# Cross-shaped window attention on one core: another order for the same instructions

## The chip, the core and the metric

The kernel runs on one core of a Trainium2 chip. The metric is device time in microseconds (us) of one execution, taken as the median of several. In the profile PE is the matrix engine (PEld its weight loads), ACT the activation engine, DVE the vector engine, POOL the GpSimd engine, and SP the engine that here only issues DMAs.

## What is computed

The input is an image of 224 x 224 tokens with 96 channels, in bfloat16. Half of the channels attend within horizontal stripes of 8 rows, the other half within vertical stripes of 8 columns. That makes 28 + 28 stripes of 1792 tokens, each an ordinary softmax attention with 48 channels.

```python
q, k, v = split(einsum('bhwc,cd->bhwd', x, wqkv))      # 96 channels each
# first 48 channels: 28 stripes of 8 rows, 1792 tokens each
ah = softmax(einsum('bqc,bkc->bqk', qh, kh) * 48 ** -0.5)
oh = einsum('bqk,bkc->bqc', ah, vh)
# last 48 channels: 28 stripes of 8 columns, 1792 tokens each
av = softmax(einsum('bqc,bkc->bqk', qv, kv) * 48 ** -0.5)
ov = einsum('bqk,bkc->bqc', av, vv)
out = einsum('bhwc,cd->bhwd', concat(oh, ov), wo)
```

## The kernel before

**Tiling.** Two stripes are worked on at once and form a pair (28 pairs, `P`). One stripe of the pair lies in partitions 0 to 63, the other in 64 to 127. The queries of a pair are cut into chunks of 512, 512, 512 and 256 (`CH`), the keys into blocks of 128. A unit is 128 keys against a chunk of queries, for both stripes.

**Units.** For a unit, PE multiplies keys and queries (line 778, `ps<-QT_sb,KT_sb`) in two steps, each of which fills one 512-column bank of PSUM. Then the scores must be exponentiated, and there are two ways:

- 984 units go to ACT: one activation (line 824) turns two banks into the tile `PT`. Then two PE steps multiply `PT` with the values (line 804, `ps<-PT,V_sb`).
- 388 units (776 banks) go to DVE: one instruction per bank (line 844) writes integers into `I_sb`, whose bits are read as bfloat16 numbers, a coarse exponential. POOL adds constants to them and makes two shifted copies, `U_sb` and `E_sb` (line 849). PE multiplies all three with the values, so such a unit has six steps on line 804.

A chunk's products pile up in one bank; DVE copies the sum into `OT_sb` (line 870), PE multiplies that with `wo` (lines 691 and 725), DVE divides by the softmax sum (lines 695 and 729), and for the vertical stripes POOL adds the horizontal half from `Ph_sb` (line 733). SP stores the result (line 760). Beside that, the next pair is projected: PE lines 535 and 637, DVE lines 549, 556 and 642, POOL lines 573, 574 and 651; SP fetches its input (lines 411 and 418).

**Tiles of the matrix engine.** All these matmuls use a 64 x 64 quarter of PE. A step works on two quarters at once, one for each stripe: either the two on the diagonal (`mode="q"`) or the two off it (`mode="v"`). A step of either kind can run beside a step of the other kind. Which kind a step is depends on the unit alone.

**Order.** Nothing is scheduled when the kernel is built. A string `SEQ` has one letter for each operation of the whole kernel, 11,330 in all. Each letter takes the next operation of its stream: `a` and `b` are the key-query steps of an ACT unit and of a DVE unit, `A` the activation, `c` the value steps of `PT`, `j` DVE's exponential, `U` and `u` the making of a `U_sb` or `E_sb` tile on POOL or, for the small letter, on DVE, `d` and `D` the value steps of the DVE unit, `f` and `e` PE and DVE work of the projections, `o`, `g`, `r`, `q`, `y` the end of a chunk from the copy to the store, `X` the fetches. A second string, `BANK`, has the PSUM bank for each tile in the order in which tiles are begun.

```python
for c in seq:                                  # Work.run, cut
    both, q = c == "p", {"p": "P", "u": "U"}.get(c, c)
    op = s.streams[q][at[q]]
    at[q] += 1
    deps = list(op.deps)
    for t in op.take + op.book:
        if t.k is None:
            t.k = int(next(digits))            # a digit of BANK
            t.after, freed[t.k] = freed[t.k], None
    ...
    s.place(op, deps)                          # next on its engine, with semaphore waits
    for t in op.give:
        freed[t.k] = [op]
```

So `SEQ` sets the order on each engine, and with `BANK` it sets which earlier operation a step must wait for before it may write into a bank. An engine takes its instructions in that order, and one that waits for a semaphore holds up those behind it on its engine.

Of the kernel before, what the change touches and what calls it, by code (L numbers as in the profile page):

```python
# [23 lines left out]
def ndc(P, c):  # L24
# [4 lines left out]
    "HiIxIihIiHiIhiiiihIiHiiihxIiiiIhiIiixhhxhxhxhhihHhxihhHhhhhhexhHhhxefHfxHfeexeaaxefAaxeafxAeaaxcebcAajabVccAja"  # L29
    "accbexdAacjacbdAjbcacajxbUAacacjbAjbcacajbxUAacjacbddAjacxacffAUeacacebeDAcaejacDAeacuacfAaafcecAecaacfoAaaeff"  # L30
    "cAceaadkgdfAkfradrXadbdeAdfaDaDejbcfcAcjaUcaXcbecAfadadjdfdfAaDeaDUbDXDfAjdadacebcAdcXdajadbdcADucacacDjbAUcac"
    "ajcbcAccjcaadobdADaDajbffdfAjdaUbadedfAcjacacfcecAbacUacegjcAbcacardjbdAdardadVddjdADbDaDjaDbcAdUcjacacbcdAcja"
    "cacDbDAoaUdadjgdAadarDdrbdDAcdjabUadcDjcAaaccbcDcjbAacacjUccgcAaoadrdbrDgADadarjdfdUAdarcacfecAgacaecfcdAUraDr"
    "aDDbDeAfcacajdbdAdaedadjdbkdAckadjUadbDcDAXXjacaccbcAjcbaaccUjcccAfadoadffADfaDeadbdUeAdgjdacacbrcAarcacfjcdbA"
    "UceacadfjdfAadbdadjbfAXcacaeDUdDdDAXjdadafDcADceabacDUcjAcbacacjbcAcoaacjbAgadadrjfUdfADfaDraddfedAaceacbfVcAe"
    "cacajcbdAdjbadaUddjbAddacajcdDbADaDjaDcbUcdAjacacbccDAjabaccDjUbdAacadjdbcAjadadcbocdAUDdadjagDdAcrDgracacDrcA"
    "brcUacacjcccAaoaddbDgAajdaUdfdrdArbDacaecfcAcjagacUcreADbDaDarDfcAdajdadfdeAUdDadacedcAdbdadjaDbcAXXjackacUbcc"
    "AjbacaccjcccAaadokdbUDAjbadaddgjdbAafrDjacffAUracacecfbcAcaejcacfcAdaudadffeAXdfadeaddDAXbdafjacdDAdeabaDDDjcb"
# [12 lines left out]
    "cjbAcDcajcacDcAagcUoacrbArdaadjgdbdAdarjDagDArdaUcarcfrcAcacaecbcfcAjDaDaDebDAadadjfddfAdeaUdacdcedAbdadjaDbDc"
    "AXXjackacUbccAjbcacaccjcfAaadodfkDfAUbDaedadgdjAdfacacerbcrAacUacjcbdfdAjadadbdeddAacjbdacDdjAXabUaDDdjDbAXcDj"
    "aDabcjcAfacUaccfcfAaceaccccbAoaadUdfjDAadadedffAadaDfbfUceAcacaecfcAceadajdbdVAdjbaDaDDjbADDacacjUdbddAjacgadc"
    "rcAbrcacacdjcUbAcacjacdbDAoadadjcgAUbadrajddcdADdrabadDjDcADgUacarcbrcAacacjcbccAcjaUadodbADajDadggdArbdradUac"
    "rjbcAdadardfdAcjacacfecUAcacaebfccAjadaddDedDAadafbdeDAXXDDDjackacUbcAcajcacbcccAjcfaadokdfUAdfadaedbdgcAjDaDa"
    "dfrdbArdUadaejdbdfAcjcacacbecAdcacajbdcdAXDjaUbaDdjDbAXDDaDjabccAjcacaUcffAcfcaeacccAcboadaUdfjdAgadaedffAdfra"
    "DraDcfUcAeabacecfcAcaeacjcbcAacVjbDaDDjbAdadadjbdUAadjbdaDdcjdcAbcacjaccdUAdbacajbcDDAaoaddjbDAgUDadardjdcdAcd"
    "radabcDAgjDUcacacrbcrAacacjcccAbodaUadjDgbDAardjadfddAragacUecbcAacrjacfccAracadefdUdAdaeaDDfDADDeabadDjbkAddU"
    "dadjabcdcAXXjacaccbcAajcakcbcccjcAUfadaodffAdadeadfgdAcrbecraDaDjfcAUcadeadbdfAdfjadadbcAcfjcacabecAXdUcaDjabd"
    "DdAXDjbadajDDDAcbUcacjacfcAcaceaccbcAoaUaddfjfAgfadeaddfdAraDraDVcfecAabaceccjbAcaUdajdbdAdajdadbDdADjbDaUDacj"  # L60
    "dcAbcacjacbcdAcjacaUbdcDAjbacacjcDbAdaoaddUdddjAcgcaacrcrdcAdabafcjDADDaecaUcDcbAcagjaccAroadardgUdbAdradjadbD"
    "ArDacajcbgAcUjacaccfrcAradaddfedAdfUaedacdDeAdDabaDdjbdDADakjDaUbccAXXjcacacbcAcjbacackjcccUAfadaodfcfAacaedgd"
# [872 lines left out]
```

## Time and the profile before

| | |
|---|---|
| median of 3 runs | 947.26 us (946.06 to 947.78) |
| profiled execution | 947.97 us |
| its span, first to last instruction | 945.8 us |
| PE busy | 935.8 us |
| ACT busy | 926.0 us |
| DVE busy | 883.1 us |
| POOL busy | 768.3 us |
| granted PE clock | 0.998 |

A row of groups on the page reads: line, engine, operation, tile written and tiles read, shapes, count; then the time in which at least one of the group ran, the mean duration of one in ns, and the idle time of the engine just before them with what ended it. Instructions of one engine overlap: the next begins while the last one drains, so durations add up to more than busy time. PE's ends are modelled, and a busy PE can still have one of its two tile pairs empty. A row of the waits reads: engine and tile that waited, what released it, us in total, times, the longest.

### The profile page before, as it was taken

The numbers are of one execution on the slowest core, as the hardware profiler recorded it, in microseconds if no ns is written. First come the engines' busy times: TensorE is split into PE (matmuls) and PEld (weight loads), VectorE is DVE, ScalarE is ACT, GpSimd is POOL, SyncE is SP. The second block draws the span as 40 slices with busy tenths as digits, with TensorE's granted clock in tenths as the row PEclk, the third lists the DMA queues.
The fourth block names the chain that finished last, engine by engine and source line by source line (L and its number), as shares of the span: only waits on it lengthen the run. The fifth ranks groups of instructions, "written<-read, shape, count | busy, mean of one in ns | idle before, by whom it ended". The sixth has DMA issues, their size and how long they took to land.

```text
span 945.8 us, 48282 instructions
## 1 busy us (share of the span) xinstructions
PE 935.8 (99%) x21770; PEld 641.5 (68%) x21770; DVE 883.1 (93%) x1755; ACT 926.0 (98%) x993; POOL 768.3 (81%) x511
## 2 busy tenths in 40 slices
PE   9999999999999999999999999999999999999997
PEld 4766767776677777667666766666776676677664
DVE  8999999999999999999999999999999999999994
ACT  7999999999999999999999999999999999999996
POOL 3789787888898887888888988887888787888883
PEclk9999999999999999999999999999999999999999
DMA  8804422440442243054210534545364544451112
GB/s 141 138 5 71 72 45 29 71 64 11 71 71 38 37 71 61 14 71 71 50 25 12 91 59 57 90 78 81 50 90 74 82 65 67 80 83 31 31 21 45
DMA packets 253254, 57.09 MB, mean 60 GB/s; under 512 B 252936, under 2 KB 252936, under 8 KB 253048
## 3 DMA queue, kind: packets, MB, share of 16 engines
q1 hardware_dynamic: 251464, 53.47, 36.0%
q8 instruction: 170, 2.79, 1.2%
q10 hardware_dynamic: 1584, 0.55, 0.3%
q14 instruction: 36, 0.29, 0.1%
HBM read 19.13 MB, written 28.21 MB: 50 GB/s over the span
## 4 chain that ended last, share of the span: by engine, by line
PE 97%; DVE 1%; DMA 1%; ACT 0%; issue 0%; POOL 0%; POOLq 0%; ACTq 0%
PE ps L804 50%; PE ps L778 36%; PE ps L535 5%; PE ps L637 4%; PE ps L691 1%; PE ps L725 1%; DMA w_sb<-in_wqkv_dram 1%; DVE I_sb L844 0%; ACT PT L824 0%; PE ps L602 0%; DVE out_sb L736 0%; PE ps L634 0%; POOL out_sb L733 0%; POOLq L302 0%; PE ps L529 0%
## 5 line engine op out<-in xcount | busy, mean ns | idle before, releaser
L824 ACT ACTIVATE PT<-ps 128x1024 bf16<-128x1024 f32 x984 | 922.0, 1034 | 7.6 <-PE ps L778 3.4
L778 PE MATMUL ps<-QT_sb,KT_sb 49*64 49x512 bf16 (+1 forms) x6272 | 740.2, 354 | 0.3
L844 DVE TENSOR_SCALAR I_sb<-ps 128x512 int16<-128x512 f32 x776 | 511.8, 684 | 21.0 <-PE ps L778 15.2
L804 PE MATMUL ps<-PT,V_sb 64*50 64x512 bf16 (+1 forms) x4496 | 498.3, 350 | 0.3 <-issue 0.3
L778 PEld LDWEIGHTS ps<-QT_sb,KT_sb 49*64 49x64 bf16 x6272 | 285.0, 105 | 144.5 <-ACT PT L824 44.4
L849 POOL TENSOR_SCALAR E_sb<-I_sb 128x2048 int16<-128x2048 int16 x168 | 319.1, 1900 | 51.8 <-PE ps L804 32.0
L849 POOL TENSOR_SCALAR U_sb<-I_sb 128x2048 int16<-128x2048 int16 x165 | 313.5, 1900 | 49.8 <-DVE I_sb L844 28.4
L804 PE MATMUL ps<-U_sb,V_sb 64*50 64x512 bf16 (+1 forms) x1776 | 245.3, 350 | 0.0
L804 PEld LDWEIGHTS ps<-PT,V_sb 64*50 64x50 bf16 x4496 | 217.7, 100 | 33.9 <-issue 1.0
L804 PE MATMUL ps<-I_sb,V_sb 64*50 64x512 bf16 (+1 forms) x1776 | 239.6, 352 | 0.2
L804 PE MATMUL ps<-E_sb,Vs_sb 64*50 64x512 bf16 (+1 forms) x1776 | 230.6, 349 | 0.0
L733 POOL TENSOR_TENSOR out_sb<-tmp,Ph_sb 128x480 bf16<-128x480 f32 (+1 forms) x84 | 85.7, 1030 | 26.2 <-DVE tmp L729 8.7
L804 PEld LDWEIGHTS ps<-I_sb,V_sb 64*50 64x50 bf16 x1776 | 80.8, 100 | 32.5 <-PE ps L804 9.3
L804 PEld LDWEIGHTS ps<-U_sb,V_sb 64*50 64x50 bf16 x1776 | 89.3, 100 | 12.5
L804 PEld LDWEIGHTS ps<-E_sb,Vs_sb 64*50 64x50 bf16 x1776 | 88.4, 100 | 13.6 <-issue 0.4
L535 PE MATMUL ps<-xa_sb,w_sb 64*64 64x512 bf16 (+3 forms) x440 | 79.9, 355 | 0.7 <-DMA w_sb<-in_wqkv_dram 0.7
L870 DVE CAST OT_sb<-ps 128x512 bf16<-128x512 f32 x112 | 69.1, 617 | 8.4 <-PE ps L804 7.9
L535 PE MATMUL ps<-xb_sb,w_sb 64*64 64x512 bf16 (+2 forms) x436 | 76.9, 348 | 0.0
L556 DVE TENSOR_SCALAR_CACHE_REDUCE KT_sb<-ps,bias 128x512 bf16<-128x512 f32 x108 | 71.6, 677 | 1.9 <-PE ps L535 1.5
L549 DVE TENSOR_SCALAR QT_sb<-ps 128x512 bf16<-128x512 f32 (+1 forms) x111 | 67.4, 616 | 3.7 <-PE ps L535 2.2
L637 PEld LDWEIGHTS ps<-w_sb,xa_sb 64*64 64x64 bf16 x1512 | 59.5, 109 | 10.9 <-DVE I_sb L844 4.0
L637 PE MATMUL ps<-w_sb,xa_sb 64*64 64x48 bf16 x1512 | 66.6, 187 | 0.1
(68 smaller groups left out, 610.4 us busy)
## 6 DMA issues: line engine op xcount, KB each, us to landing
x_blocks<-in_x_dram SPq DMA_DIRECT2D x54, 336.0 KB
out_dram<-out_sb SPq DMA_DIRECT2D x104, 42.0 KB
out_dram<-out_sb SPq DMA_DIRECT2D x208, 21.0 KB
out_dram<-out_sb SPq DMA_DIRECT2D x22, 24.0 KB
xa_sb<-x_blocks SPq DMA_TRANSPOSE x27, 5.0
xb_sb<-x_blocks SPq DMA_TRANSPOSE x27, 5.5
Ph_sb<-in_x_dram ACTq DMA_DIRECT2D x1, 336.0 KB, 3.3
out_dram<-out_sb ACTq DMA_DIRECT2D x6, 24.0 KB
```

What stands on the lines that cost most here:

```text
L535: ins = e.matmul(out_, lhsT=wt, rhs=rhs, start=i == 0, stop=startup or i == 1)
L549: return e.tensor_scalar(dst, src, QS if startup else A128, None, ALU.mult)
L556: return e.tensor_scalar(dst, src, bias[:, 0:1], None, ALU.add, ALU.add, accum_out=acc)
L637: ins = e.matmul(out_, lhsT=(xa_sb, xb_sb)[i][b][o:o + 64, 0, t0:t0 + 64], rhs=w2_sb[o:o + 64, i, wblk(P, "v"), 0:C2], start=i == 0, stop= ...
L691: ins = e.matmul(bk3[to:to + 64, s, :], lhsT=OT_sb[b][o:o + CA, blk * 64:(blk + 1) * 64], rhs=wo_sb[0][o:o + CA, :], start=True, stop=True)
L733: return e.tensor_tensor(res, tmp[t][:, 0:n, :], ph, ALU.add)
L778: ins = e.matmul(bank(t.k)[to:to + 64, i * qs:(i + 1) * qs], lhsT=KT_sb[b][64 * w:64 * w + CA, 64 * k:64 * k + 64], rhs=QT_sb[b][64 * w:64 ...
L804: ins = e.matmul(bank(k_.slot.k)[to:to + CP, 0:qs], lhsT=V_[o:o + 64, k, :], rhs=rhs()[o:o + 64, h * 512 + i * qs:h * 512 + (i + 1) * qs], ...
L824: a = wk.add("A", Op("act", ACT, lambda e: e.activation(split(PT[i % NPT]), two(ts), ACTF.Exp, scale=LN128), qs_ + pt_free.get(i - NPT, [] ...
L844: ds.append(wk.add("j", Op("dve", 0.6, lambda e, t=t, at=at: e.tensor_scalar(I_sb[y][:, at:at + 512], bank(t.k), one, 0.0, ALU.add, ALU.ma ...
L849: fn = lambda e, dst=dst, c=c: e.tensor_scalar(dst[:, 0:m], I_sb[y][:, 0:m], float(c), 1.0, ALU.add, ALU.mult)
L870: k.evac = wk.add("o", Op("dve", 0.07 + qs / 960, lambda e, k=k, b=P % 2, q0=q0, qs=qs: e.tensor_copy(OT_sb[b][:, q0:q0 + qs], bank(k.slot ...
```

## The change

Only the two strings differ. The letters are the same and as many, but for two tiles `U_sb` or `E_sb` that DVE makes instead of POOL (57 small `u` instead of 55). The first 12 and the last 4 letters agree. Two lines of the diff of `SEQ` show its kind:

```diff
 SEQ = (
-    "HiIxIihIiHiIhiiiihIiHiiihxIiiiIhIiiixhhxhxhxhhihHhxihhHhhhhhexhHhhxefHfxHfeexeaaxefAaxeafxAeaaxcebcAajabVccAja"
...
+    "HiIxIihIiHiIihiiihIiHiiihxIiiiIhIiiixhhxhxhxhhihHhxihhHhhhhhexhHhhxefHfxHfexeeaaxefAxaeaxfAeaaxcecbAaeaVccAjba"
...
```

On PE, just after the start: rows of line 778 are key-query steps, of line 804 value steps, and x2 is one step (a matmul for each stripe). Before:

```order
L778 MATMUL ps<-QT_sb,KT_sb 64x512 x4
L804 MATMUL ps<-PT,V_sb 50x512 x2
L778 MATMUL ps<-QT_sb,KT_sb 64x512 x2
L804 MATMUL ps<-PT,V_sb 50x512 x2
L778 MATMUL ps<-QT_sb,KT_sb 64x512 x6
L804 MATMUL ps<-PT,V_sb 50x512 x4
L778 MATMUL ps<-QT_sb,KT_sb 64x512 x4
L804 MATMUL ps<-PT,V_sb 50x512 x4
```

After:

```order
L778 MATMUL ps<-QT_sb,KT_sb 64x512 x4
L804 MATMUL ps<-PT,V_sb 50x512 x4
L778 MATMUL ps<-QT_sb,KT_sb 64x512 x6
L804 MATMUL ps<-PT,V_sb 50x512 x4
L778 MATMUL ps<-QT_sb,KT_sb 64x512 x6
L804 MATMUL ps<-PT,V_sb 50x512 x4
L778 MATMUL ps<-QT_sb,KT_sb 64x512 x2
L804 MATMUL ps<-I_sb,V_sb 50x512 x2
```

The two key-query steps of an ACT unit now mostly follow each other (523 of 984 units; 105 before), where a value step stood between them before (840 units before, 375 now). Over the whole of PE the places where the next step uses the other tile pair become fewer: runs of one step between such places go from 5287 to 2937, runs of two from 912 to 1396, runs of three or more from 176 to 595.

On PE, near the end, a place of before where four value steps stand ahead of two key-query steps (the names as above, `U_sb` and `I_sb` being tiles of DVE units):

```order
L778 MATMUL ps<-QT_sb,KT_sb 64x512 x4
L804 MATMUL ps<-PT,V_sb 50x512 x4
L804 MATMUL ps<-U_sb,V_sb 50x512 x2
L804 MATMUL ps<-I_sb,V_sb 50x512 x2
L778 MATMUL ps<-QT_sb,KT_sb 64x512 x4
```

And a place near the end of after:

```order
L778 MATMUL ps<-QT_sb,KT_sb 64x512 x6
L804 MATMUL ps<-PT,V_sb 50x512 x2
L804 MATMUL ps<-E_sb,Vs_sb 50x512 x6
L778 MATMUL ps<-QT_sb,KT_sb 64x512 x2
L804 MATMUL ps<-PT,V_sb 50x512 x4
L778 MATMUL ps<-QT_sb,KT_sb 64x512 x4
```

Such rows of several steps in a line are rare in before and common in after.

On POOL, the first tiles that it makes (with their buffer numbers; `Vs_sb` and `half`, `ksb` belong to the projections). Before:

```order
L651 TENSOR_SCALAR Vs_sb0<-V_sb0 128x1400
L849 TENSOR_SCALAR U_sb0<-I_sb0 128x2048
L849 TENSOR_SCALAR E_sb0<-I_sb0 128x2048
L849 TENSOR_SCALAR U_sb1<-I_sb1 128x2048
L573 TENSOR_TENSOR half<-ksum1 128x2
L574 TENSOR_TENSOR ksb1<-half 128x1
L849 TENSOR_SCALAR U_sb2<-I_sb2 128x2048
```

After:

```order
L651 TENSOR_SCALAR Vs_sb0<-V_sb0 128x1400
L849 TENSOR_SCALAR U_sb0<-I_sb0 128x2048
L849 TENSOR_SCALAR U_sb1<-I_sb1 128x2048
L849 TENSOR_SCALAR E_sb1<-I_sb1 128x2048
L849 TENSOR_SCALAR E_sb0<-I_sb2 128x2048
L573 TENSOR_TENSOR half<-ksum1 128x2
L574 TENSOR_TENSOR ksb1<-half 128x1
```

Which tiles fall to DVE changes, and POOL's tiles stand otherwise among the small steps of the projections. On SP the fetches of a pair now stand between single stores instead of behind all 24 of a pair. ACT runs the same activations in the same sequence; only what they wait for differs.

More of the change, by code (lines that the diff above doesn't have):

```diff
@@ L34 @@
[L34 to L38, printed above, removed]
@@ L129 @@
[L129 to L131 removed]
+    "HiIxIihIiHiIihiiihIiHiiihxIiiiIihIiixhhxhxhxhhihHhxihhHhhhhhexhHhhxefHfxHfexeeaaxefAxaeaxfAeaaxcecbAaeaVccAjba"
+    "acxcjbdAcajacbdAjbcacaxjbUAcacajbAjacacbxAfuacacjdAdcaxecaUbDDAjbacacjbAacjacUfAaceacefAeaeaecbcAacjacfoAuaaec"
@@ new lines @@
+    "cAadadbDfADjadXUadefdAdbafeacfjfAgcaecXakcbcrAckarDaDjbDfAcaceacjXcfbAaDUaddDdDeAUXdfafjafdAddaeacbdcdAjacaccb"
+    "cdcjbAacajcbcAaoadUdfDjADaadedffAgfdardaUecfAcracabcefcAaDaDeDVjbDADcaaddjdbcDdAajacdcdAddacaUUAacbccjcacbdcdA"
+    "cjacabodddaAdjadDgDAcdrdabraAdcDjcDbaajccfUcAcecaabcAcccjgadadrofUdAdaarddgcerbDAaacjDbcAdacjagdrdAbDaUdrabjcc"
+    "caArcaDfDjAddbUaecadAcDjdabadjcdcfAXXcUaeackbcDAcjbDaakcjcccAfaaDodbjdfAaUDaddfdcbAadaecgccaadAcjcbrrAfdUejdaa"
+    "dbdfAjcaadeDAbXcDcdcaUjaDbDdAXcjfafafcAedUbaaccdjAcDDbacjacccbAoaUacjbAgdaarjdfdAdadrUabdeADfDaajccfbfAdaedadf"
@@ new lines @@
+    "UAjdedaadcdbccdDDAaacdbcjaVAjcabcAdDDajUaccbAcDccjacacfDcAceaoUadADbDdaajcbcfdjdAddaeadUcgcdAgracracDDcAracrba"
+    "cUcccjaAbdaodfdAjdadadegbADDjacrabccAcjagacdcrbAUdarajddcAcrbadadfDjcAUbaecadDdjDDabdAajcdcfcAXaXceaUbcDcADjba"
+    "acjcccAfadoabddAfUDajadDfdgbAceaacrcckdbjAkdaarUAdjacdbcadfddcjbAacabecjDdUAdDXDajacDfAXcafafecfAUcdecabacAdDj"
+    "bcDcaajcbAcaUoacAjgbDaadrrdfDdAacajcfdfAedfabUaecdfAjdaaceAbddfadadVdddAcjaDceaDDbudADaacjbcdcAcajaccccbADuaac"
+    "cDbjcUAcajaddDdAobaaccjddbDdAajadgccAdragcUraADDrccbacarcjcccAbaUdaodfjAddedaaDbdgADcaajccrAbcfdrjacadcdAbacae"
@@ new lines @@
+    "dUfdjdAcbcaeaccdcAdjagaUDrDDAdardbjaDcAXXbajcaccfDAcUcaebacocfADjabadfjdfAdadaedkgkbADrcajcadAbrccaaDjbAddUjaU"
+    "ccbadfjAddDbaaedjbdAcDaXjuDaDdccfAXaaffecfAecdaacUbcAdjcDbacjaDbcAacajccUcAobaaddjdfAdaDaebDffUAdfjcaabdefAcac"
+    "jecacUAbcfdaaDeddbdjAbaadjcddccAjdaabDdDcAgaDVaccjcDdAracraDcAcbcadjabUdcUddAajaDDfocAdaaedcgcUAdcdragracDrccD"
+    "bcAaracjcccAUbaadodfjdADadeabddgcAajbaDccrjAbcccaarcfdUdAjadabcdefADDaaeDjUdbADjdaagcbcArajadcddrcAXXdbjaacbUD"
+    "cDAaacjcbcccAjcfaadodffaAaeddgdbAcrUDcajabkArDkccaUcjabdcfAjcadaecbdAddajbUacfdccjAXaedabfAXcfafjadUDDeAddabac"
@@ new lines @@
+    "DDjbAdccjaabUcDcAajcaoDcAbcbjagadUddraaAjdfrddADDaaebcfcfAUjcfacaedcbacdAajdfbddAaVacDddAddcajUecDaDdbcAjDaUca"
+    "cbcDcaAcjabcDccAjbaadDdoAfUdadaeccjAdDdgadacDbrrdAcUaaDcjcbcAjcacagccAcraoarbdAddgadadjbdArjUDDaagcrcbAcrcaajc"
+    "fAcddraUadebdfADaddjacDbeAaDajddcAcDfcaaUdcdfAXXceaacDcbecDAajbacccccAjafkadodfbDAajdaDbddfkAdajcUagcecAfcUaac"
+    "crcberfDDaAjaceAbDDcaUacfjdfAdXbjaadbdddfAXjadadcdecdAaUbacjDcbAccDajacbcAcjaUacboAaadjdfdbdaAdeUafdfAjDfabaDe"
+    "cfAjdaacUVebdcAcfdaaDdeadjDaAbdcdjDdADbcaacjcAcdbgjaUarcAccDcdcraacbcADcajcadUbdocaAcajdgdddADraraddUDfAcgacaD"
@@ new lines @@
+    "ercDcAcabcraUcAjcccabadodfADdaajddbdacaeADjbcfAjDDDaaceggdUAaDadrrbdcrdAajarccUdbfcaaAedccjdbAddjaacbcdcAXbXka"
+    "jaDcUjcDAbakcacjcbccAcfjaaddfoADfaUcDeabdcgAdjaadbcrAdfdacarUcejbAcfdjdaaedddbAdacaUccjbAXccjdabaDcdAcXjdfafUa"
+    "fDfAeccaDeaDDAbDcaajcUcbAcoaacjbAgddarajfdfAdfrUdaadbcbeaAajDDfcAjcacacbecfAdcaaceaDdbdbjAaddjVcdddAjaacdDUDAb"
+    "jcaaDbcAjcudacaccDDcaAcdaoadUdbADdjadDcdgAdcdarafrcUAcaceabjDcDAcbaacjccccUAagobdadrjdAdbaadrdfDADjcaacgceUcAb"
+    "agrcjacdcaArdadfrcraAUDabddedfAcaeDaDdDjbcbAkjdaaAcXXjddcabaDjccbDAakccjacbccAjUcfaadodfbUaAadjddfcDbAeaDadfjd"
@@ new lines @@
+    "bcAUaceacjfAdddaeabccgAjdaaUccrcbdADdaXraDdjDDfAXafafUdccbdAeUaaDjccAcbDcajabccAccajacboAdadjadfdAgaedaUdfDfAr"
+    "DfcaraccfeAdaeadddfAddeaabddcbcjAdajVcacbccAcaUajbcDAcdjDbaacjDDcDbAUaacjDcbAccajaAcdobcDUaDadfjcAdgdeaacddrAd"
+    "cacraUDbjDcbdAcjcaaccgcAoaUadbrdDrgAddarjaccAdbardacfjcAgaaUDcfrceAcaceacfdAdDraadedbbUdjcdaAadDjDbdDAajdabckj"
+    "kAXXdcbacaDjcbcAjDaUacbcccAjcfaadodfUdAbdajdadfAcbeaDacDgjcbAUccaajcfrdAdedrabaddfcdAjcaUabeacAXcjcdadDAbXDcjd"
+    "fUafafDdaADbeaDcjcDcAbaUjaccccbAoaacjbAgdaadrjfUDdadAraddffeADfcaabecfUAdjddaadbedfAcaecajccbDAbaadcjUAddjccca"
@@ new lines @@
+    "DbacjDbADaVcjadcbjccdcaaAccUbDDAoaaddjgaDAadrddrgcUAdDrdfrcaaAbdaeDacccDjcbaUAjacccbccAjcaadobdUAdaaddjggDrADb"
+    "racrajcAUdcbrcaacfAdjcadabddefAdjcaadDceDdAbUaaDjDdAbddDjaabcDAXXcjUcacabccfaccAjacecccAafoDadbdfDadAjUadkfdgA"
+    "ceacacbrjAcckcbaUracdfeAdjaaddbdfDddaAjabeDfcUAXacajbfcfAXadajddecDbAjacDacUbDcaAjcbacccdjcDAaabocUfaAddjagedf"
+    "AdfadrDadrfDAcbeaaccfjAcdacVaedbcfUAdacjaddedbAdacUjaccbcAdajaDcDdbcAaajcDdDcbAcaUcjacDbDAoadadjdgDAaadUDrrbAd"
+    "dcdajadbDcDAcjacgUacbrcAcracacjcccAaadodfUdAdgaeadDbArdDajgaccUrAcbaarjccdbdcaAadrdfjAdDDbaaeDDfAdjcaceacdUdbA"
@@ new lines @@
+    "jUdaadcfcADDXbXeacacbjkAckacacbjcccAcjfaaoddfDbAdaajddfUdgaAcearbcDcfArcaaecdjbcfAUcddaadjdeAbddcaajbcddAcXajb"
+    "acUjDcAdXfafafcDcbAaDaejDcUDbcDcAajacAccboaaddfjUbdAeadadffAfjaabeAdDDcfUaaccbjcceAcajaccfbcDDAeaacjbDDADdjaag"
+    "dDudbAdadradUddcccAaacjrbccdbAajadcVjAcUbadadobAjcDaaDdddjdcAagUdargDcrdAaaDccrcrbAcaaccjcccAobUaadjddgbAdDrad"
+    "adjfDAragUacecfcAcrceaacfArddaDadfedbAdaecacDjAcbDkaajcddAdbadjaUbkAXDXcdDDacjabccbAccajUacjccAcfaodadfDfADeUa"
+    "dagdcAbrcadradfjccbaAaeccjbccUaAdbajdfdAdjaaedddDbdaDAXjaDDfcfUAXafaeADbDdccUaabjcAccjcdabacccccAjbaadodfUAdaj"
@@ new lines @@
+    "adddfDfeAfDaabecfUcAdadjacbecfAdaeaddjddAVgacraccrbAdDajaDDcdbAjcuaacccbcDDAUjaaccDbdAcjacacodADbddaadjdbAcdDj"
+    "UaabDccjdAbaaDdjccAbaacjUccgcAcragraccAroaadrdgUbAdDadadrjDAdbragajcfcUAcraecacccAcbaraccfdjDAeaadbddfAjdacaeb"
+    "ddUADdafjadDDAXDXedbDacacbckUjaAcacjcbccjcAfaodadfdfAadadekbcUdgAcDaajfDrcecAbracacbdjfAUddjaadcdebdcAdajadbdA"
+    "XDjDaUbaDdDjAXcDfafafDAccbecaUaccbjcAajcacccAobcaadUdfjADdfaedaddffADaeagcfcrAVrbacacecAcaacfjcbcdAUaDeajddbAj"
+    "adcbdadjAUcddbDDaaDjbcAcjacabcjccDAUcDaabodbdAajaddgcAdjbaUaDDdrdAdjDraaddcccbjAcacUacbDcAjagacccrcAraadbUoddf"
@@ new lines @@
+    "dDADjaaedgdbAacrcjaUcfcAcracaccebfAdajddadfedAaUgdaDdrDDAedarbadDdjcAbaUDjabcAXcXckDcjaabcccAcjbaaccjcfAaoaddf"
+    "DfAecDaacbgcdbjAddUkUaadjfAceddarardfcbAdecaaccfjAcfbaadcjfUAXddDeaaDdbAdXDjdaabDcDjDUbcAjaacccfcaAacceAbocUca"
+    "addfjfAdfadaeddfAVgDaaercDfcAeccarabbcUAcajadadddaADDbjdddjbAdajaUcdcDcAbcajacbcDAdjcaabcUDccAcacjaDboaAdajddg"
+    "dDdAUraabDcrddAjabaDccDjbccaaAUcjbcAjcdaagcrcccAradUaodbdfAdjadeadDggAaDacrrUcfAcDarecabDAdrcbaaDjDcfAddjaadDd"
+    "ddeAUbcaajcdbAcddajfaceDAXXcbUccajacbcAaccjacccfAobadadjdfADfkadeaDdgbAdcrjUaabcrkccAcUaqadcfdjbdAaejaddfAacec"
@@ L165 @@
+    "47635014673541067540157645012764501267450126740156741054673105743601563450162345106324106325410643251024350127"
+    "45310274532017345210725401724571025467012654017465210425641025460132546310245301725437012543017234510452371450"
+    "125431062345601423501432546123451203475012754013245710234510624365"
 )
```

208 lines of the change are left out of this document (79 added, 129 removed).

## Prediction

> **What bounds the kernel now.** I read the page's busy times and its chain first, then the groups, then the waits. In a group's row the numbers after the bar are busy us, mean ns of one, and idle us before it.
>
> ```profile
> span 945.8 us, 48282 instructions
> ...
> PE 935.8 (99%) x21770; PEld 641.5 (68%) x21770; DVE 883.1 (93%) x1755; ACT 926.0 (98%) x993; POOL 768.3 (81%) x511
> ...
> PE 97%; DVE 1%; DMA 1%; ACT 0%; issue 0%; POOL 0%; POOLq 0%; ACTq 0%
> ...
> L824 ACT ACTIVATE PT<-ps 128x1024 bf16<-128x1024 f32 x984 | 922.0, 1034 | 7.6 <-PE ps L778 3.4
> ```
>
> The chain runs along PE, but PE and ACT are both full to 98% or more, so the chain alone does not say which one sets the time. For ACT its own row of the tile PT and its timeline give the answer. The timeline merges neighbours: start, length, and how many.
>
> ```profile
> L824 ACT ACTIVATE PT<-ps x984: 1017/1024/1191, 9.6 to 937.2; 128x1024 bf16<-128x1024 f32 x197
> 913.46 24.85 ACT L824 ACTIVATE PT<-ps 128x1024 bf16<-128x1024 f32 x27
> 9.57 13.40 ACT L824 ACTIVATE PT<-ps 128x1024 bf16<-128x1024 f32 x14 [0.89 <-PE ps L778]
> 937.20 1.11 ACT L824 ACTIVATE PT<-ps 128x1024 bf16<-128x1024 f32 x1
> ```
>
> Near the end 27 activations take 24.85 us. One lasts 1.02, so their starts are (24.85 - 1.02) / 26 = 0.917 us apart: that is ACT unhindered. At the start 14 of them take 13.40 us, which is 0.952 apart. From 9.57 to 937.20 + 1.11 = 938.31 are 928.7 us, and 983 x 0.917 + 1.02 = 902.4. **ACT is held up by 26.3 us** in all. The page's 7.6 us of idle time is only the part in which nothing was draining. So the span is 9.6 of start, 902.4 of ACT, 26.3 of hold-ups and 7.5 of end. An order cannot change the 902.4; it can change the 26.3.
>
> Who holds it up? The waits:
>
> ```profile
> PEld ps L778 <- ACT PT L824: 44.4, 188, 0.5
> POOL E_sb L849 <- PE ps L804: 32.0, 32, 3.6
> POOL U_sb L849 <- DVE I_sb L844: 28.4, 34, 2.2
> PEld ps L778 <- DVE I_sb L844: 22.6, 100, 0.5
> DVE I_sb L844 <- PE ps L778: 15.2, 53, 0.7
> ACT PT L824 <- PE ps L778: 3.4, 8, 0.9
> ```
>
> Only PE's key-query steps (line 778) release ACT. PE in turn waits 188 times for ACT to give a pair of banks back, 100 times for DVE to give one back, and never for POOL in these rows; POOL waits for PE and DVE. It is a ring: an activation frees two banks, PE fills them, the activation after next reads them. Where PE has too much between two fillings, ACT stands; where it has too little, PE stands, with all that is queued behind it.
>
> **The change, term by term.** *The steps of PE.* The change mostly makes steps of one tile pair follow each other. What that costs depends on whether a step of the other pair can start while several of the first still wait ahead of it. The second place of the order above, where four value steps stand ahead of two key-query steps, is this in the trace:
>
> ```profile
> 930.09 0.38 PE L804 MATMUL ps<-PT,V_sb 64*50 64x512 bf16 x2
> ...
> 930.10 0.40 PE L778 MATMUL ps<-QT_sb,KT_sb 49*64 49x512 bf16 x2
> 930.30 0.38 PE L804 MATMUL ps<-PT,V_sb 64*50 64x512 bf16 x2
> ...
> 930.34 0.38 PE L778 MATMUL ps<-QT_sb,KT_sb 49*64 49x512 bf16 x2
> 930.52 0.38 PE L804 MATMUL ps<-U_sb,V_sb 64*50 64x512 bf16 x2
> ```
>
> The value steps start 0.216 us apart (930.09, 930.30, 930.52), each as its tile pair comes free. The first key-query step, written behind four of them, starts at 930.10, ahead of three. Through the whole trace I find no start that needs more than three waiting matmuls per tile to be passed, and many that need one to three. So a row of steps on one pair costs nothing as long as the other pair's next step is within three. Laid end to end in their order at 0.216 us per 512 columns, both pairs filled, three passable, each value step behind the one of its chunk that it must follow, the steps of before come to 889.8 us and those of after to 887.3. The runs of three and more (176 before, 595 after) are thus nearly free: this term is -2.5 us if PE sets the time, 0 if ACT does.
>
> The Trainium skill says otherwise: "TensorE: Matmul & The Clock Gate", in Part 3 on packing small matmuls, has matmuls start and end strictly in program order, with only weight loads pulled ahead. This trace differs at 930.10 against 930.30, and the measurement decides here; by the rule the sum would be the last rival below.
>
> *The hold-ups of ACT.* In the same laying-out, the work of PE between the ends of two successive fillings for ACT exceeds 0.917 us in 313 of 983 gaps before and in 303 after; the excess adds to 69.6 and 65.9 us, 5% less. The other way round, I counted the steps of PE that would come to their bank or tile before it is free, taking 1.03 us for an activation (row of L824) and 0.69 for DVE's pass from these rows:
>
> ```profile
> L844 DVE TENSOR_SCALAR I_sb<-ps 128x512 int16<-128x512 f32 x776 | 511.8, 684 | 21.0 <-PE ps L778 15.2
> L849 POOL TENSOR_SCALAR E_sb<-I_sb 128x2048 int16<-128x2048 int16 x168 | 319.1, 1900 | 51.8 <-PE ps L804 32.0 <-PE ps L778 4.4 <-DVE U_sb L849 3.0
> L849 DVE TENSOR_SCALAR U_sb<-I_sb 128x2048 int16<-128x2048 int16 x29 | 20.0, 688 | 0.1
> ```
>
> 929 steps of before do so, by 120.6 us together; 843 of after, by 112.8, 6% less (those behind ACT go from 69.0 to 63.1, those behind DVE from 51.4 to 49.6). Both counts are of the order alone and overstate the 26.3, but both fall by a twentieth. 5 to 6% of 26.3 is 1.4 to 1.7; I take **-1.5 us**. Of the -2.5 of the steps I take half, **-1.2**, since in part of the kernel PE waits for ACT anyway. Bounds for both together: -4.2, and 0 if the gaps only change places.
>
> *POOL and DVE.* Two tiles move from POOL (1.900 us each) to DVE (0.688): -3.8 on POOL, +1.4 on DVE. DVE has 945.8 - 883.1 = 62.7 us free, POOL more; I take **0**, with +1.4 as the bound if DVE's place is just then on the ring. The value steps of E_sb and U_sb come nearer to POOL's making of them: counted in steps of PE from the letter of the tile to its first use, none of 1332 is under 1.9 us in before and 11 of 1324 are in after, together 5.3 us short; under 2.5 us it is 24 before and 59 after. That is a new wait for PE, with the next key-query steps queued behind it. It is at 0 in my sum, because a letter's place need not be the time at which POOL comes to it, and is priced as a rival.
>
> *SP.* The fetches of a pair's input move ahead of some stores. A fetch lands in 4.0 to 6.2 us:
>
> ```profile
> DMA to landing us min/median/max: 4.0/5.3/6.2
> L418 SPq DMA_TRANSPOSE xa_sb<-x_blocks x27: 1226/1475/2277, 13.0 to 843.0; - x27
> L418 SPq DMA_TRANSPOSE xb_sb<-x_blocks x27: 1379/2294/3622, 14.3 to 844.4; - x27
> ```
>
> From its letter to the first projection that reads it lie at least 11 us of PE's steps in before (the lowest hundredth) and 14 in after: cost 0. If this cover went, PE would stand for up to 6.2 us a pair. The projections' places among the steps stay nearly as they were, and so do the start (first 12 letters the same, the first activation at 9.57) and the end (the last activation, eight steps of PT, copy, `wo`, stores, 7.5 us): 0.
>
> **The sum.** -1.5 - 1.2 + 0 = -2.7 us against the profiled execution's span of 945.8: 943.1. Its time is 947.97, so 2.2 lie outside the span, and it is 0.7 above the median of 947.26. Against the median the forecast is 947.26 - 2.7 = 944.6 us. About 0.2%, or 1.9 us, is what a measurement of this kernel tells from no change.
>
> **The rivals.**
>
> *Much faster.* If the new order meets the real ends of the activations and not only on average, the hold-ups could halve: 26.3 / 2 = 13, 934 us. For it speaks that nothing bounds the gain before 26.3; against it, that both counts fall only by a twentieth. Chance 0.12.
>
> *No change.* The gaps move and their sum stays; or the fewer early steps of PE only let PE stand less, which costs nothing now. 945.4 to 949.1. Chance 0.14.
>
> *Slower by POOL's tiles.* Place: value steps of E_sb and U_sb that come under 1.9 us behind the making of the tile. Price: 5.3 us from the 11 that are short, and up to 59 x 2.5 less their distances, 23.9 us, if POOL comes to its tiles 0.6 late; in the middle about +9, 956 us. It decides from the point at which PE waits for POOL by some 4 us, as the gain is then gone. For it: POOL waits 32.0 us for PE and 28.4 for DVE, so it often starts late. Against: the same counts show 24 near ones in before, and no wait of PE for POOL is among the long ones. Chance 0.24.
>
> *Slower because less can be passed.* If in rows of steps only one waiting matmul per tile can be passed, the same laying-out gives 907.4 before and 921.8 after, +14.4: 961.7 us. Against it are starts like the one at 930.10. Chance 0.11.
>
> *Strictly in order.* With none passable it is 942.9 and 1024.6, +82: 1029 us. The first projection stands in the chain (start, length, count):
>
> ```profile
> 6.48 1.13 PE ps L535 x9
> ```
>
> Before would then need 942.9 us of PE from 6.5 on, to 949, past the span's end at 945.8; the trace refutes it. This is what the skill's page named above would give. Chance 0.03.
>
> **The numbers.** Forecast, some 2 to 9 us faster: chance 0.36. With 0.12 for much faster that makes 0.48 faster, 0.14 the same, 0.24 + 0.11 + 0.03 = 0.38 slower. The forecast's own range is 938 to 945.3, and its point 944.6. The whole range goes from 934 (hold-ups halved) to 962 (one passable); left out are the strict order, the upper end of POOL's case and gains over a half, under 0.2 together.
>
> **What would show it.** If I am right, the timeline of ACT after has some 24 to 25 us of hold-ups where now there are 26.3, the wait of L778 for ACT stays near 44 us, matmuls of line 778 start ahead of value steps that stand in front of them in rows of four, and PE's waits for POOL stay under 2 us. If PE's waits for U_sb or E_sb on POOL come up among the first rows, it is the third rival. If PE has no more waits than now and yet takes longer, with one tile pair empty behind rows of three, it is the fourth. The prediction is wrong in its main step if the order's count of early steps and over-full gaps says nothing about the hold-ups: then ACT's 26.3 changes by much more than a twentieth either way, with the same waits as now.

## The result, and the profile after

The changed kernel takes 944.8 us (median of 6 runs, 943.48 to 945.13); the kernel before, run beside it, 948.49 (6 runs). The ratio is 0.9967, with a 95% interval of 0.9954 to 0.9979: faster by 0.3%, some 3 us. The forecast was 944.6. It was built on 947.26, the median of three runs of before; the other three lie at 949.2 to 949.7. The profiled execution took 944.72 us; its span is 2.9 us shorter than before's 945.8.

The page of the changed kernel: span, busy times, the chain's shares, and ACT's group.

```profile
span 942.9 us, 48262 instructions
...
PE 931.8 (99%) x21770; PEld 646.6 (69%) x21770; DVE 884.5 (94%) x1757; ACT 922.4 (98%) x993; POOL 764.5 (81%) x509
...
PE 97%; DVE 1%; ACT 1%; issue 0%; POOL 0%; POOLq 0%; ACTq 0%; DMA 0%
...
L824 ACT ACTIVATE PT<-ps 128x1024 bf16<-128x1024 f32 x984 | 918.4, 1039 | 6.1 <-PE ps L778 3.5
```

The page looks as before. As in the prediction, ACT's timeline tells more: the first activations and the last ten of the changed kernel.

```profile
9.88 14.30 ACT L824 ACTIVATE PT<-ps 128x1024 bf16<-128x1024 f32 x15 [0.89 <-PE ps L778]
924.15 9.39 ACT L824 ACTIVATE PT<-ps 128x1024 bf16<-128x1024 f32 x10
```

ACT now works from 9.88 to 924.15 + 9.39 = 933.54, 923.7 us, where it took 928.7. Less the unhindered 902.4, **the hold-ups fell from 26.3 to 21.3 us**, by 5.0. That is more than the whole gain. The start came 0.3 later (9.57 to 9.88; in the kernels below it lies anywhere from 9.25 to 10.21), and from the last activation to the end of the span it is now 942.9 - 933.5 = 9.4 us where it was 7.5. So -5.0 + 0.3 + 1.9 = -2.8.

The waits of the changed kernel (total us, times, longest), and from before one row that the prediction did not show:

```profile
POOL U_sb L849 <- DVE I_sb L844: 53.5, 55, 6.4
PEld ps L778 <- ACT PT L824: 41.6, 167, 0.7
PEld ps L778 <- DVE I_sb L844: 17.2, 72, 0.5
DVE I_sb L844 <- PE ps L778: 12.9, 46, 1.2
POOL E_sb L849 <- PE ps L804: 6.2, 6, 1.6
ACT PT L824 <- PE ps L778: 3.5, 10, 0.9
PEld ps L804 <- PE ps L804: 1.2, 6, 0.3
```

```profile
PEld ps L804 <- PE ps L804: 9.3, 34, 0.3
```

PE waits less for the banks of ACT (44.4 before) and of DVE (22.6), and much less for itself. That last wait was not in my reading: a value step of one tile pair must come behind certain steps of the other pair on the same output chunk, and waits for their semaphore. Call it a handover. POOL's waits moved from PE (for `E_sb` 32.0 before, 6.2 now) to DVE (for `U_sb` 28.4 before, 53.5 now), but no wait of PE for a `U_sb` or `E_sb` tile is in the rows of the changed kernel.

**Why the end grew.** SP's stores of the last two pairs, with the POOL additions (line 733) that release the first 24 of them. Before:

```profile
911.83 0.92 POOL L733 TENSOR_TENSOR out_sb<-tmp,Ph_sb 128x384 bf16<-128x384 f32 x1
912.78 15.55 SPq L760 DMA_DIRECT2D out_dram<-out_sb  x24
928.37 15.67 SPq L749 DMA_DIRECT2D out_dram<-out_sb  x22
937.09 1.81 SPq L749 DMA_DIRECT2D out_dram<-out_sb  x1
```

After:

```profile
905.82 2.85 POOL L733 TENSOR_TENSOR out_sb<-tmp,Ph_sb 128x480 bf16<-128x480 f32 x3
908.70 15.54 SPq L760 DMA_DIRECT2D out_dram<-out_sb  x24
924.27 16.87 SPq L749 DMA_DIRECT2D out_dram<-out_sb  x22
926.45 1.89 SPq L749 DMA_DIRECT2D out_dram<-out_sb  x1
930.95 1.86 SPq L749 DMA_DIRECT2D out_dram<-out_sb  x1
```

In each kernel SP issues 46 stores without a gap from the moment the last addition of the pair before the last is done, about 0.65 us each, and the span ends 1.8 us after the last issue (944.04 to 945.8, and 941.14 to 942.9). So the end is SP's. It starts 912.78 - 908.70 = 4.1 us earlier and loses 1.2 us in the last 22 stores (15.67 to 16.87). The single rows show where: one store of before took 1.81 us, two of after took 1.89 and 1.86. At each of those times there is a packet on a DMA queue for instructions. That queue's row from 936.5 to 939.2 in before, and from 926 to 932.6 in after:

```profile
q8 instruction: 1, 0.02, 3.4%
```

```profile
q8 instruction: 2, 0.03, 2.5%
```

Not every such packet does it: three others in before and two in after, from the first of the 46 stores to the last, lengthen no store. Whose instructions they carry is not shown, so the link is one of time only. The traces of all eleven kernels below have two long stores there, like after. Those made from before have them too (e1 1.34 and 1.59 us, e5 1.24 and 1.61, e8 2.01 and 1.46, e9 1.39 and 1.61), so the single one of before is the exception, and the 1.2 us are not shown to come from the new order. In sum, -4.1 + 1.2 = -2.9, the change of the span. Of the 1.9 us by which the end grew, 1.2 are the stores; the other 0.7 is that SP's queue starts 24.8 us ahead of the end of the last activation where it was 25.5 (933.54 - 908.70 and 938.31 - 912.78).

### The profile page after: what moved, and what is told of

Read it like the earlier page. It is cut to its first block, busy times and chain, and to the rows that moved or that the text cites. A ratio compares the mean times of both kernels' runs of the same rounds, so it can differ in the third digit from the quotient of the medians.

```text
span 942.9 us, 48262 instructions
## 1 busy us (share of the span) xinstructions
PE 931.8 (99%) x21770; PEld 646.6 (69%) x21770; DVE 884.5 (94%) x1757; ACT 922.4 (98%) x993; POOL 764.5 (81%) x509
## 4 chain that ended last, share of the span: by engine, by line
PE 97%; DVE 1%; ACT 1%; issue 0%; POOL 0%; POOLq 0%; ACTq 0%; DMA 0%
PE ps L804 48%; PE ps L778 36%; PE ps L535 5%; PE ps L637 4%; PE ps L691 1%; PE ps L725 1%; ACT PT L824 1%; PE ps L396 0%; DVE I_sb L844 0%; DVE out_sb L736 0%; DVE tmp L729 0%; PE ps L602 0%; PE ps L634 0%; PE ps L496 0%; POOL out_sb L733 0%
## 5 line engine op out<-in xcount | busy, mean ns | idle before, releaser
L778 PE MATMUL ps<-QT_sb,KT_sb 49*64 49x512 bf16 (+1 forms) x6272 | 743.5, 354 | 0.8 <-ACT PT L824 0.5
L844 DVE TENSOR_SCALAR I_sb<-ps 128x512 int16<-128x512 f32 x776 | 513.5, 684 | 19.4 <-PE ps L778 12.9
L804 PE MATMUL ps<-PT,V_sb 64*50 64x512 bf16 (+1 forms) x4496 | 530.9, 350 | 0.2
L849 POOL TENSOR_SCALAR U_sb<-I_sb 128x2048 int16<-128x2048 int16 x174 | 330.5, 1900 | 88.0 <-DVE I_sb L844 53.5
L778 PEld LDWEIGHTS ps<-QT_sb,KT_sb 49*64 49x64 bf16 x6272 | 281.5, 105 | 138.3 <-ACT PT L824 41.6
L849 POOL TENSOR_SCALAR E_sb<-I_sb 128x2048 int16<-128x2048 int16 x157 | 298.3, 1900 | 34.7 <-DVE U_sb L849 12.3
L804 PE MATMUL ps<-U_sb,V_sb 64*50 64x512 bf16 (+1 forms) x1776 | 260.8, 350 | 0.0
L804 PE MATMUL ps<-E_sb,Vs_sb 64*50 64x512 bf16 (+1 forms) x1776 | 251.6, 350 | 0.0
L804 PE MATMUL ps<-I_sb,V_sb 64*50 64x512 bf16 (+1 forms) x1776 | 249.8, 352 | 0.0
L637 PE MATMUL ps<-w_sb,xb_sb 64*64 64x48 bf16 x1512 | 66.1, 186 | 0.4 <-issue 0.4
```

The source lines that it names most:

```text
L637: ins = e.matmul(out_, lhsT=(xa_sb, xb_sb)[i][b][o:o + 64, 0, t0:t0 + 64], rhs=w2_sb[o:o + 64, i, wblk(P, "v"), 0:C2], start=i == 0, stop= ...
L778: ins = e.matmul(bank(t.k)[to:to + 64, i * qs:(i + 1) * qs], lhsT=KT_sb[b][64 * w:64 * w + CA, 64 * k:64 * k + 64], rhs=QT_sb[b][64 * w:64 ...
L804: ins = e.matmul(bank(k_.slot.k)[to:to + CP, 0:qs], lhsT=V_[o:o + 64, k, :], rhs=rhs()[o:o + 64, h * 512 + i * qs:h * 512 + (i + 1) * qs], ...
L844: ds.append(wk.add("j", Op("dve", 0.6, lambda e, t=t, at=at: e.tensor_scalar(I_sb[y][:, at:at + 512], bank(t.k), one, 0.0, ALU.add, ALU.ma ...
L849: fn = lambda e, dst=dst, c=c: e.tensor_scalar(dst[:, 0:m], I_sb[y][:, 0:m], float(c), 1.0, ALU.add, ALU.mult)
```

## The experiments

Changes in us below are ratios against the kernel before, times 948.3, or against the changed kernel's 0.9967 for kernels made from it. In the diffs of `SEQ` one place of many is shown. PE's waits in the table are counted step by step, by a rule of mine: a step waits where it starts with the release of a semaphore, after its own tile pair is free and the steps ahead of it are out of the way (handovers are counted from 15 ns on; "other" are starts over 60 ns late for which no semaphore was found). The sums of the main kernels, with the hold-ups (first activation to the end of the last, less 902.4):

| kernel | hold-ups | PE waits for ACT | DVE | POOL | handover | other | sum |
|---|---|---|---|---|---|---|---|
| before | 26.3 | 42.9 | 52.0 | 0 | 24.1 | 2.6 | 121.6 |
| after | 21.3 | 46.4 | 48.1 | 0 | 19.7 | 2.3 | 116.6 |
| e1 | 31.7 | 37.0 | 65.9 | 0 | 24.0 | 3.7 | 130.6 |
| e2 | 28.9 | 61.6 | 45.5 | 0 | 19.2 | 3.9 | 130.2 |
| e3 | 59.7 | 52.2 | 86.2 | 0.8 | 28.0 | 7.3 | 174.4 |
| e4 | 88.7 | 111.3 | 93.0 | 0 | 24.9 | 4.0 | 233.3 |
| e5 | 26.0 | 45.1 | 53.0 | 0 | 19.9 | 4.7 | 122.6 |
| e9 | 26.8 | 45.1 | 53.1 | 0 | 18.1 | 4.6 | 120.8 |
| e10 | 63.4 | 42.4 | 47.6 | 79.9 | 25.1 | 2.3 | 197.4 |

The sum ranks the kernels as the hold-ups do, but for before, e5 and e9, which lie within 2 us; no single column does. In size the two differ: against before the sum grows by 9.0 for 5.4 us of hold-ups in e1, and by 75.8 for 37.1 in e10. From before to after both fall by 5.0. PE's steps are the same in all these kernels, so the sum is nearly the lost time told over again: it says where time is lost, not why.

It also depends on the rule of counting. The profile's own wait rows of PEld, all added, come to 135 us in before, 106 in after, 133 in e1, 119 in e2, 117 in e3 and 173 in e4: by them e1 and e3 wait less than before, though they are 5.5 and 33 us slower. For the size of chance differences there are e8 and e7 below, which keep the orders of before and after but for two stores: their hold-ups are 25.1 and 20.7 us, and their rows of L778 for ACT and DVE differ from those of before and after by at most 0.9.

**e1, grouping alone.** The kernel before with key-query steps set side by side.

```diff
-daddfedAdfUaedacdDeAdDabaDdjbdDADakjDaUb
+adddfedAdfUaeadcdDeAdDaabDdjbdDADakjaDUb
```

> The kernel before with 812 places of PE's order changed from a, X, a to a, a, X (the two filling steps of one ACT tile side by side, as the new order has them), nothing moved on any other engine. Counted on the order with PE's steps laid end to end: the stretch from one filling to the next exceeds ACT's 917 ns by 70.1 us in sum (before 69.6, changed kernel 65.9); steps that PE would reach ahead of their operand would be early by 109 us in sum (before 121, changed kernel 113). Theory 'evenness' (hold-ups of ACT follow the stretches that are too long): no change, 948.5 within 1 us, hold-ups of ACT near 26 us. Theory 'earliness' (they follow what PE reaches too early): -11 us of it where the change took 8, so about -4 us, 944 to 946. Theory 'side by side' (the grouping itself brings the gain): about -3 us, 945.5. Theory 'one or no waiting matmul can be passed': steps end to end go from 907.4 to 909.2 with one, from 942.9 to 1007.3 with none: +2 or +64 us.

Measured: 1.0058 (1.0045 to 1.0070), 5.5 us slower, hold-ups 31.7. Earliness and "side by side" asked for a gain; evenness for none. One passable step asked for a loss of 2, but the trace has starts that pass two and three. The strict order would have cost 64 and is out. The rule of the Trainium skill ("TensorE: Matmul & The Clock Gate", Part 3) that matmuls start strictly in program order does not hold for these steps. The waits of e1 show where the price is paid, though not why: fewer for ACT's banks (44.4 before), more for DVE's (22.6).

```profile
PEld ps L778 <- ACT PT L824: 36.8, 152, 0.5
PEld ps L778 <- DVE I_sb L844: 27.5, 111, 0.5
```

**e2, the grouping undone.** The changed kernel with 427 units apart again.

```diff
-aceacdUdbAjUdaadcfcADDXbXeacacbjkAckacac
+aceacdUdbAjUdadacfcADDXbXeacacbjkAckacac
```

> The changed kernel with 427 places of PE's order put back from a, a, X to a, X, a; nothing moved on any other engine. Stretches too long by 65.8 us in sum (changed kernel 65.9), early by 130 us (113). 'Evenness': no change, 944.8 within 1 us. 'Earliness': +17.7 us of it, 2.3 times what the change took away, so +4 to +8 us, 949 to 953. 'Side by side': about +1.5 to +3 us, 946.3 to 948. 'None can be passed': -21 us (1024.6 to 1003.8 end to end).

Measured: 1.0022 (1.0014 to 1.0031), 5.2 us slower than the changed kernel. Here the wait is for ACT:

```profile
PEld ps L778 <- ACT PT L824: 51.4, 194, 0.8
PEld ps L778 <- DVE I_sb L844: 15.5, 64, 0.5
```

Earliness fits e2, but not e1. Set against before, the two read: grouping alone +5.5, the rest of the change nearly alone (e2) +2.1, both -3.1. Neither part alone brings the gain. The two are not quite the parts of the change, though: e1 brings 812 units together, 918 with those that were, where the change has 523.

**e3 and e4, the counts of the prediction, moved on purpose.** Some 4,070 of the 11,330 letters differ from the changed kernel; the counts that should not matter are held.

```diff
-defAdjcaadDceDdAbUaaDjDdAbddDjaabcDAXXcj
+defAdjcaDacdedbAaUaDdjdbADdDDjaaDbcAXXcj
```

> The changed kernel with neighbouring PE steps exchanged until PE would reach steps ahead of their operand by 59 us in sum in place of 113, while the stretches between fillings (64.7 us too long in sum against 65.9), the steps end to end (885.9 against 887.3) and what they are if only one waiting matmul can be passed (921.8, the same) are held. Other engines' orders unchanged. 'Earliness': a third to all of ACT's 21.2 us of hold-ups go, 930 to 940 us. 'Evenness' and 'side by side': no change, 944.8 within 1.5 us.

> The same with the exchange made the other way: PE would reach steps ahead of their operand by 222 us in sum in place of 113; stretches too long by 66.2 us (65.9), steps end to end 884.4 (887.3), with one passable 921.9 (921.8). 'Earliness': hold-ups of ACT up by 10 us or more, 952 to 975 us. 'Evenness' and 'side by side': no change, 944.8 within 1.5 us.

Measured: 1.0348 and 1.0647, 36 and 64 us slower than the changed kernel. Every theory fails on e3, earliness worst: it has half the early steps and nearly three times the hold-ups. e4 went the way that earliness asked, but far past its 952 to 975 us (1009.85). The waits of e3:

```profile
PEld ps L778 <- ACT PT L824: 24.8, 100, 0.5
DVE I_sb L844 <- PE ps L778: 24.5, 81, 1.4
ACT PT L824 <- PE ps L778: 16.3, 58, 0.9
```

What was counted did go: the wait for ACT's banks on line 778 fell from 41.6 to 24.8. (The step count has all waits of PE for ACT at 52.2, more than the 46.4 of after.) But DVE's string was left as it was, and DVE now waits 24.5 us for its fillings (12.9 in the changed kernel); PE's waits for DVE go from 48.1 to 86.2. The sequence in which PE's steps feed DVE is nearly the same (65 of DVE's 1391 passes over a bank stand ahead of one that PE feeds earlier, 58 in the changed kernel), so what the exchange upset must be the spacing; that is argued, not shown. My count lets DVE's pass follow its filling at once, as if DVE were free; in the changed kernel it is busy for 94% of the span, and it takes its instructions in order.

**e5 and e6, exchanges chosen on a plan in which engines wait.** The plan sets each operation at the time at which its engine, its inputs and its bank allow it. Of e5, and then e6:

```diff
-jdAgadaedffAdfraDraDcfUcAeabacecfcAcaeac
+jgAdadardffAdfeaDraDcfUcAeabacecfcAcaeac
```

```diff
-DgjcbAUccaajcfrdAdedrabaddfcdAjcaUabeacA
+DgjcbAUccaarcfjdAdedrabaddfcdAjcaUabeacA
```

> The kernel before with 137 exchanges of two neighbouring steps on PE or on DVE, each taken only where a plan that lets every engine wait for what it needs (durations of the trace of before, up to three waiting matmuls passed, also with two, and with some operations late) ends earlier by it; everything else as before. The plan's hold-ups of ACT fall by 3 us (26.9 to 23.8). Theory 'where the waits close their loop' (ACT frees a bank, PE refills it, ACT waits for the refill): 2 to 4 us faster than before, 944.5 to 946.5, hold-ups of ACT near 23. Theory 'any disturbance of a tuned order costs' (812 and 427 exchanges without a reason cost about 5.5 us each way): slower than before by 1 to 2 us.

> The changed kernel with 98 such exchanges, each taken by the same plan with the durations of its own trace. The plan's hold-ups fall by 0.6 to 1.5 us. 'Where the waits close their loop': 0.5 to 1.5 us faster than the changed kernel, 943.3 to 944.3. 'Any disturbance costs': 1 us slower, about 946.

Measured: e5 0.9997 (0.9989 to 1.0006), no change; e6 0.9955 (0.9944 to 0.9967), 1.1 us faster than the changed kernel, with intervals that overlap. The plan's 3 us in e5 did not come, nor did the 1 to 2 us of loss. By the table handovers fell by 4.2 us, and the waits for ACT, DVE and others rose by 5.3. By the rows of L778 the waits for ACT and DVE fell a little (to 43.6 and 21.2), so where the time went is not shown.

**e9, handovers alone.** The kernel before, with exchanges only at its 78 long handovers.

```diff
-aacrcrdcAdabafcjDADDaecaUcDcbAcagjaccAro
+aacrcrdcAdabafDjcADDaecaUcDcbAcagjaccAro
```

> The kernel before with 64 exchanges of neighbouring PE steps, put only where the trace of before shows a value step of one tile pair waiting over 60 ns for steps of PE's other tile pair on the same output chunk (78 places, 18.3 us in sum); the waiting step goes one or two steps later, or the last awaited one earlier. In the changed kernel all such waits over 15 ns are 19.7 us where before has 24.1. Theory 'the handover waits are the gain' (they fell by 4.4 us and ACT's hold-ups by 5): half of them go here, 3 to 6 us faster than before, 943 to 945.5. Theory 'waits move' (a wait that is taken away comes back at ACT's or DVE's banks, as in the relaid kernel before, where 4.2 us of them went and 3.2 us came back there): within 1 us of 948.5.

Measured: 1.0007 (0.9998 to 1.0015), no gain. The waits of e9, to be set against before's 9.3, 44.4 and 22.6:

```profile
PEld ps L778 <- ACT PT L824: 45.8, 194, 0.5
PEld ps L778 <- DVE I_sb L844: 23.0, 102, 0.5
PEld ps L804 <- PE ps L804: 3.5, 14, 0.3
```

The waits were taken away where I aimed, 6.0 us by the table, and 5.3 came back at banks of ACT and DVE and elsewhere; in the rows above, 5.8 went and 1.8 came back. Taking handovers away is thus not by itself a gain, though they also fell in the changed kernel.

**e10, POOL makes every tile.** All 57 small `u` made large.

```diff
-eAbcDcjaacccAbudacacbcjdAdaUDcacjDDAoaad
+eAbcDcjaacccAbUdacacbcjdAdaUDcacjDDAoaad
```

> The changed kernel with all 57 tiles that DVE makes of I_sb made by POOL instead: +108 us of work on POOL (busy 873 of 943 us), -40 us on DVE; the order is otherwise the same. Theory 'POOL has time and PE never waits for it': within 3 us of 944.8. Rival 'slower by POOL's tiles', of the prediction: tiles come late, PE waits for POOL by 10 us or more, 955 to 1000 us.

Measured: 1.0375 (1.0360 to 1.0389), 39 us slower than the changed kernel. The rival's mechanism is real. Busy times and waits of e10:

```profile
PE 944.1 (96%) x21770; PEld 644.4 (66%) x21770; DVE 857.1 (87%) x1700; ACT 927.2 (94%) x993; POOL 872.7 (89%) x566
```

```profile
ACT PT L824 <- PE ps L778: 39.2, 52, 2.2
PEld ps L804 <- POOL E_sb L849: 38.2, 37, 2.2
PE ps L804 <- POOL E_sb L849: 23.7, 31, 1.9
```

POOL still has 982.3 - 872.7 = 110 us without work, and PE waits 79.9 us for it by the table. ACT stands behind PE: its wait for line 778 goes from 3.5 to 39.2 us, nearly the whole loss.

**e7 and e8, two stores moved from SP to ACT**, in the changed kernel and in the kernel before; in `SEQ` two late `y` become `Z`.

```diff
-store("act" if (s if last else wf and c == 2) else "sp", ...)
+store("act" if (s if last else c == 2 and (wf or s >= 2)) else "sp", ...)
```

> The changed kernel with two of the last 22 stores issued by ACT after its last activation in place of SP; nothing else. Theory 'SP's queue of 46 stores sets the end' (about 0.645 us each, without a gap from the last addition of the pair before): 1.3 us faster, 943.5. Theory 'the chain of ACT, PE and DVE sets the end': no change, 944.8 within 0.5 us.

> The same two stores moved to ACT in the kernel before. There SP's last store was issued 2.4 us after DVE's last output, in the changed kernel 4.4 us after. 'SP's queue sets the end': 1.3 us faster, 947.0 where before is at 948.3. 'The chain of ACT, PE and DVE sets the end': no change.

Measured: e7 0.9946 (0.9933 to 0.9958), 2.0 us faster than the changed kernel (the intervals overlap by 0.0004); e8 0.9988 (0.9979 to 0.9997), 1.1 us faster than before. SP's last stores in e7, ACT's in e7, and SP's in e8:

```profile
923.99 15.26 SPq L749 DMA_DIRECT2D out_dram<-out_sb  x20
```

```profile
933.13 5.18 ACTq L749 DMA_DIRECT2D out_dram<-out_sb  x8
```

```profile
927.00 15.34 SPq L749 DMA_DIRECT2D out_dram<-out_sb  x20
```

Their last issues end at 939.25 and 942.34, and the spans are 941.0 and 944.1: 1.8 us behind SP again. SP's queue sets the end in both kernels.

**e11, e6 and three stores on ACT.**

> The changed kernel with the 98 exchanges of e6 and with three of SP's last stores issued by ACT after its last activation. SP's queue then ends with 19 stores and ACT's with 9: by the queue theory 1.9 us off the end where two stores took 1.7, until ACT's own queue is as late; with the 1 us of e6, 941.5 to 942.5. If the chain of PE, ACT and DVE set the end, 943.9 as in e6.

Measured: 942.93 us, 0.9938 (0.9924 to 0.9952), the fastest median of all but above the 941.5 to 942.5 expected, with an interval that lies below the changed kernel's; from e7 it does not differ beyond the intervals. SP's and ACT's last stores:

```profile
924.60 13.81 SPq L749 DMA_DIRECT2D out_dram<-out_sb  x19
```

```profile
933.54 5.86 ACTq L749 DMA_DIRECT2D out_dram<-out_sb  x9
```

SP is done at 938.41, ACT at 939.40, and the span ends at 941.2: the bound has passed to ACT's queue. In this execution the hold-ups are 21.3 us, as without the exchanges, so the 1 us of e6 is not established.

## Why the prediction was right or wrong

**The sum was right, its terms were not.** -2.7 stood against -2.9 in the profiled executions (-3.1 by the ratio), out of -5.0 for the hold-ups, +0.3 for the start and +1.9 for the end, where I had -2.7 for the first and 0 for the others. Two errors nearly cancel, which is luck. So is part of the match of 944.6 and 944.8: from the 948.49 of all six runs of before, the same -2.7 gives 945.8.

**Hold-ups of ACT: direction right, size half.** Forecast for hold-ups and steps together was -2.7 with a bound of -4.2; measured is -5.0, a fifth of them and not a twentieth. The step that failed is the one from counts that fall by a twentieth to hold-ups that fall by a twentieth; the sign "24 to 25 us of hold-ups" came out at 21.3. The prediction named this as the way in which its main step would be wrong, "ACT's 26.3 changes by much more than a twentieth" (its addition "with the same waits as now" did not come true: the waits changed as well). e3 shows that the count of early steps does not even give the sign: with half of them the time rose by 36 us. The counts see each step against an engine that is always free. The sum of PE's waits by my rule did fall by 5.0, but that is where the time was, not what set it free, and the order alone did not show it.

**Which edit makes the 5 us is not settled.** Grouping alone loses (e1), the rest nearly alone loses (e2), handovers alone give nothing (e9). That the gain is in how the parts fit is the reading left, and it is not shown. An exchange of the sequences of one engine alone, PE's new one with DVE's old one, was not tried: each would wait for the other in a circle. Nor were the other parts of the change taken by themselves: the new `BANK` (2,916 of its 3,366 digits differ), POOL's order with the two moved tiles, and SP's fetches (SP's new order would fit the kernel before without such a circle).

**Passing of waiting matmuls: right.** At this place of the changed kernel PE's order is four value steps and then a key-query step of the other pair, which starts at 922.09, ahead of three of them:

```profile
921.88 0.40 PE L804 MATMUL ps<-I_sb,V_sb 64*50 64x512 bf16 x2
922.09 0.38 PE L778 MATMUL ps<-QT_sb,KT_sb 49*64 49x512 bf16 x2
922.12 0.38 PE L804 MATMUL ps<-I_sb,V_sb 64*50 64x512 bf16 x2
922.33 0.38 PE L804 MATMUL ps<-U_sb,V_sb 64*50 64x512 bf16 x2
...
922.55 0.38 PE L804 MATMUL ps<-U_sb,V_sb 64*50 64x512 bf16 x2
```

In the traces of before, after and e1 to e4 no start needs more than three to be passed. The two rivals on this point are out: the long rows did not cost what they said.

**POOL's tiles: right for this change, and nearer than I saw.** No wait for `U_sb` or `E_sb` came up. e10 shows that the rival was no phantom; there the letters keep their places and POOL has 14% more work.

**The end at 0: wrong.** I laid the end out as steps behind the last activation (PT, copy, `wo`, stores). It is SP's queue, fed since 908.7. No wait for a fetch came up among the rows, as forecast; the stores were the part of SP that I had not priced. One more blocked store than in before cost 1.2 us, and since the kernels made from before have two as well, the order is not shown to be its cause.

**"The wait of L778 for ACT stays near 44":** it is 41.6, and DVE's fell too, from 22.6 to 17.2.

## What to carry to other kernels

Where several engines are full and each takes its work in order, a count of conflicts on the order of one engine does not give a time, not even its sign. Sums of waits do not give the cause either: by one way of counting they tell the time over again, by another they rank the kernels wrongly. Judge a reordering by a run. Total idle time of an engine (178 us on POOL) is not room at the place where its result is needed. Follow the end back along every queue, those that only issue DMAs too: two stores on another queue were worth 1.1 and 2.0 us, where the new order of 11,330 operations brought 3.1.

## What was not expected of the hardware

- Three of the 92 last stores of before and after took 1.81 to 1.89 us to issue where their neighbours take about 0.65, each at a packet of about 0.02 MB on the instruction queue q8; five other such packets held up none. In the last stores of all thirteen traces there are 25 that took 1.15 to 2.01 us, each within 0.4 us of such a packet, and 27 more such packets that held up none.
- Two queues issue side by side at nearly full rate: in e7 ACT's eight stores took 5.18 us (0.65 each), and eight of SP's in the same stretch took 5.39 (0.67 each).
- Up to three waiting matmuls of one tile pair were passed by the other, and never more, in the six different orders of before, after and e1 to e4.
